# Split weights of a gated linear stage kept in DRAM and read back; the first block by plain products; no arithmetic on GpSimd

## The chip, the cores and the metric

The kernel runs on one core of one Trainium2 chip. The metric is device time in microseconds (us), the median of several executions; one more execution was taken by the hardware profiler. The engines are named as in the profile: PE (TensorE matmul), PEld (its weight load), DVE (VectorE), ACT (ScalarE), POOL (GpSimd) and SP (SyncE, which issues most DMAs here).

## What is computed

Linear attention with a per-head norm, then a mixture of eight experts of which each token takes one, then a gated linear unit. 4608 tokens of 512 features go through all of it, in float32.

```python
def _attn_ref(q, k, v, g_norm):
    kv = np.einsum('bhsd,bhse->bhde', k, v)
    out = np.einsum('bhsd,bhde->bhse', q, kv)
    rms = np.sqrt(np.mean(out * out, axis=-1, keepdims=True) + 1e-06)
    return (out / rms * g_norm).astype(np.float32)
...
def _moe_ref(x, modality_id, w_gate, modality_bias, w1, w2):
    logits = x @ w_gate + modality_bias[modality_id]
    e_idx = np.argmax(logits, axis=1)
    ...
        h = np.maximum(x[mask] @ w1[e], 0.0)
        out[mask] = gate_w[mask, None] * (h @ w2[e])
...
def _moe2_ref(x, w_gate, w_val, w_out):
    gate = 1.0 / (1.0 + np.exp(-(x @ w_gate)))
    val = x @ w_val
    return (gate * val @ w_out).astype(np.float32)
```

The last function is the stage that the change is about, the gate/value stage: w_gate and w_val are 512 x 1536, w_out is 1536 x 512.

## The kernel before

**Stages.** Attention comes first (to about 160 us). Then the expert stage, `run(0, NSURE)`: 22 items of one or two tiles of 128 tokens, four steps each, in which PE multiplies by pieces of w1 and w2 that ACT and DVE have split just before. Beside it, `Decode` turns the three float64 weights of the last stage into float32 and stores them in DRAM as `w_d`. Then the gate/value stage: 6 blocks (NB) of 768 tokens in two halves of 384 columns (HC), and in each block 12 units (NJ), one for each 128 of the 1536 inner features. Units are numbered 0 to 71. Unit 0 runs at the end of the expert stage (`gv_first`), before the branch at L954; the others run in the loop at L1151.

**Splits.** A float32 product is made as three float32r products. Each operand is split into hi (ACT copies it to float32r) and lo (a subtract of hi from the operand); then hi·hi, hi·lo and lo·hi are added in PSUM.

**A unit.** `glu_unit` (L627) makes gate and value of 128 inner features for 768 tokens by a scheme with seven products of half the depth in place of eight. That needs sums of the operands: of the weights (`sum_w`, four sums on POOL, L616) and of the tokens (`y_steps`, four sums on POOL, L578), and sums of the results, which DVE makes from PSUM (L638). A product is six matmuls of 384 columns (L634 to L636): 42 for a unit. Weights for unit s + 1 are split during unit s, in four groups (`split_wg`: ACT L624, DVE L625); the raw rows come from `w_d` by one read of 512 KB for each unit (L986). The split weights of a unit are used once and made again in each of the six blocks.

**Output steps.** `ready_o` (L1002) splits 128 rows of w_out, read from `w_d` (ACT L1010, POOL L1011), and the finished product gm (ACT L1015, DVE L1016, `gl`); `out_step` (L1020) then issues nine matmuls of 512 columns. In units 1 to 12 there is one for each unit, from unit 13 on two; the last 14 stand at the end, behind unit 71.

**Order.** The order is written out by hand. `glu_unit` calls `at(p)` after each of its products, and `prepare(s, p)` (L1095) holds what every engine does there for later units; each engine keeps to the order in which its instructions are issued. In units 10 and 11 of a block, the next block's y operands are made in seven steps (s1 to s7: ACT L573, DVE L574, POOL L578). In block 0 the last eight of the 36 decoding jobs run too (`Late`, units 2 to 9; their last add is on POOL, L1080). SP issues its DMAs in program order, and one that waits holds up all behind it.

**The way into the stage.** The last 16 steps of the expert stage (`later(q, ...)`, q = 0 to 15) also prepare unit 0 and block 0: rows of y are read, each row's gate is gathered by POOL (`number`), ACT multiplies by it (`weigh`, steps 5 to 7), PE transposes (`flip`, steps 6 to 11, ACT copies to `yraw`), POOL sums the weights (step 6), ACT and DVE split them (`group0`, steps 11 to 14), and `steps0` makes the seven y operands in steps 12 to 15: POOL copies hi (L571), DVE subtracts lo (L574), POOL sums (L578).

Of the kernel before, what the change touches and what calls it, by code (L numbers as in the profile page):

```python
# [73 lines left out]
def attention_moe_glu_kernel(  # L74
# [487 lines left out]


    y11, y12, y21, y22 = (yraw[:, 2 * k:2 * k + 2, h, :] for k in range(2) for h in range(2))
    free_y, Y = [], {}

    def split_y(b, n, src, first=False):

        hl = free_y.pop(0)
        if first:  # L570
            nc.gpsimd.tensor_copy(out=hl[0], in_=src)  # L571
        else:
            nc.scalar.activation(out=hl[0], in_=src, func=ACTF.Copy)  # L573
        nc.vector.tensor_tensor(out=hl[1], in0=src, in1=hl[0], op=ALU.subtract)  # L574
        Y[b, n] = hl

    def sum_y(out, in0, in1, op):
        nc.gpsimd.tensor_tensor(out=out, in0=in0, in1=in1, op=op)  # L578

    def y_steps(b, first=False):  # L580


        def s1():
            split_y(b, 3, y22, first)
            sum_y(y22, y22, y12, ALU.subtract)

        def s2():
            split_y(b, 1, y11, first)
            sum_y(y12, y12, y11, ALU.subtract)
            sum_y(y11, y22, y11, ALU.add)  # L590

        def s3():
            split_y(b, 6, y11, first)

        def s4():
            split_y(b, 7, y22, first)

        def s5():
            split_y(b, 2, y21, first)
            sum_y(y21, y21, y11, ALU.subtract)  # L600

        def s6():
            split_y(b, 4, y21, first)

        def s7():
            split_y(b, 5, y12, first)
# [583 lines left out]
```

## Time and profile before

| | us |
|---|---|
| median of 3 executions | 1651.11 (1649.55 to 1652.71) |
| the profiled execution | 1653.95 |
| its span, first to last instruction | 1652.2 |
| PE busy | 1484.2 |
| DVE busy | 1211.9 |
| ACT busy | 839.1 |
| POOL busy | 748.4 |
| mean granted clock of PE | 0.955 of full speed |

Times in the rows below are us from the span's start. Matmuls are pipelined: the duration of one is its latency, so the pace of PE is read from the distance between starts. "Busy" counts instructions that overlap once. Releasers of a wait are inferred from semaphores.

### The profile page before, as it was taken

How to read it: one execution, taken by the hardware profiler on the slowest of the kernel's cores; microseconds unless marked ns; L12 is line 12 of the kernel's file. 1: busy time of each engine (PE TensorE's matmuls, PEld its weight loads, DVE VectorE, ACT ScalarE, POOL GpSimd, SP SyncE). 2: the span in 40 equal slices, each digit the busy share in tenths (PEclk: the TensorE clock that was granted, in tenths of full speed). 3: DMA queues.
4: the chain of work that ended last, by engine and by line, in shares of the span. 5: the costliest groups of instructions: out<-in, count | busy, mean ns of one | idle time of the engine just before them, and what ended most of it. 6: DMA issues, size and time to landing. Idle time of an engine off the chain costs nothing.

```text
span 1652.2 us, 25283 instructions
## 1 busy us (share of the span) xinstructions
PE 1484.2 (90%) x9361; PEld 1350.6 (82%) x9361; DVE 1211.9 (73%) x1766; ACT 839.1 (51%) x1492; POOL 748.4 (45%) x777
## 2 busy tenths in 40 slices
PE   6993999999999987788789989997999799989996
PEld 6882899999999976677679888987998798879984
DVE  2658778888887877577677786778777877877764
ACT  3755555555555566244344454454455445544443
POOL 1121122222222234455466665666566667565545
PEclk9986999999999998799799999999999999999999
DMA  9957687758866773323223323332333233222312
GB/s 298 338 192 267 189 302 270 255 187 320 282 225 234 255 279 133 110 90 135 96 79 127 116 77 107 116 108 74 116 112 106 77 122 119 87 83 96 116 52 101
DMA packets 122816, 266.29 MB, mean 161 GB/s; under 512 B 17728, under 2 KB 38464, under 8 KB 121664
## 3 DMA queue, kind: packets, MB, share of 16 engines
q1 hardware_dynamic: 108480, 228.01, 41.3%
q0 software_dynamic: 11488, 36.27, 6.2%
q8 instruction: 75, 1.23, 0.3%
q10 hardware_dynamic: 2720, 0.35, 0.2%
q14 instruction: 53, 0.43, 0.1%
HBM read 245.24 MB, written 40.32 MB: 173 GB/s over the span
## 4 chain that ended last, share of the span: by engine, by line
PE 70%; DVE 8%; POOL 7%; issue 5%; ACT 4%; DMA 4%; SPq 0%; ACTq 0%; POOLq 0%; another core or an unknown queue 0%; DVEq 0%
PE gv L634 9%; PE gv L636 8%; PE gv L635 8%; PE ac L1031 4%; PE ac L1032 4%; PE ac L1030 4%; PE py L810 4%; PE py L809 4%; PE py L811 4%; PE ph L772 4%; PE ph L771 4%; PE ph L770 4%; DVE wt L625 2%; PE kv L248 2%; PE ops L285 2%
## 5 line engine op out<-in xcount | busy, mean ns | idle before, releaser
L625 DVE TENSOR_TENSOR wt<-rows,wt 128x512 fp32r<-128x512 f32 (+1 forms) x284 | 235.0, 832 | 109.7 <-ACT wt L624 108.1
L1011 POOL TENSOR_TENSOR wol<-wo,woh 128x512 fp32r<-128x512 f32 x144 | 193.1, 1343 | 262.7 <-ACT woh L1010 260.7
L616 POOL TENSOR_TENSOR rows<-rows 128x256 f32<-128x256 f32 x288 | 250.1, 889 | 37.0 <-DMA rows<-w_d 24.5
L634 PE MATMUL gv<-half,wt 128*128 128x384 f32 x590 | 204.8, 347 | 29.3 <-DVE u L638 10.7
L636 PE MATMUL gv<-half,wt 128*128 128x384 f32 x590 | 200.9, 340 | 0.3 <-DVE wt L625 0.3
L635 PE MATMUL gv<-half,wt 128*128 128x384 f32 x590 | 200.4, 340 | 0.0
L819 POOL DMA_INDIRECT y_d<-y,sidx x40 | 48.0, 1201 | 299.3 <-issue 130.8
L1031 PE MATMUL ac<-wol,gh 128*128 128x512 f32 x432 | 172.7, 400 | 10.3 <-POOL wol L1011 10.3
L1016 DVE TENSOR_TENSOR gl<-gm,gh 128x384 fp32r<-128x384 f32 x144 | 168.8, 1173 | 14.3 <-ACT gh L1015 14.3
L1032 PE MATMUL ac<-woh,gl 128*128 128x512 f32 x432 | 172.3, 399 | 0.0
L1030 PE MATMUL ac<-woh,gh 128*128 128x512 f32 x432 | 169.7, 393 | 0.1
L624 ACT ACTIVATE wt<-rows 128x512 fp32r<-128x512 f32 (+1 forms) x284 | 158.1, 570 | 18.2 <-POOL rows L616 12.7
L770 PE MATMUL ph<-xh,w1h 128*128 128x256 f32 x576 | 166.6, 289 | 0.8 <-ACT xh L753 0.8
L772 PE MATMUL ph<-xl,w1h 128*128 128x256 f32 x576 | 163.8, 284 | 0.0
L771 PE MATMUL ph<-xh,w1l 128*128 128x256 f32 x576 | 163.7, 284 | 0.0
L634 PEld LDWEIGHTS gv<-half,wt 128*128 128x128 f32 x590 | 112.9, 191 | 41.3 <-DVE gm L638 15.6
L666 ACT ACTIVATE s<-s 128x384 f32<-128x384 f32 x71 | 37.4, 526 | 194.5 <-DVE s L638 194.5
L810 PE MATMUL py<-w2l,hh 128*128 128x512 f32 x320 | 126.8, 396 | 0.8 <-DVE w2l L732 0.8
L809 PE MATMUL py<-w2h,hh 128*128 128x512 f32 x320 | 126.7, 396 | 0.1
L811 PE MATMUL py<-w2h,hl 128*128 128x512 f32 x320 | 125.4, 392 | 0.0
L635 PEld LDWEIGHTS gv<-half,wt 128*128 128x128 f32 x590 | 113.0, 192 | 2.2
L636 PEld LDWEIGHTS gv<-half,wt 128*128 128x128 f32 x590 | 112.7, 191 | 1.0 <-DVE wt L625 1.0
(258 smaller groups left out, 3790.6 us busy)
## 6 DMA issues: line engine op xcount, KB each, us to landing
half<-in_moe_w_dram SPq DMA_DIRECT2D x24, 2048.0 KB
rows<-w_d SPq DMA_DIRECT2D x72, 512.0 KB
wo<-w_d SPq DMA_DIRECT2D x144, 256.0 KB
w1r<-in_moe_w_dram SPq DMA_DIRECT2D x11, 2048.0 KB
w2r<-in_moe_w_dram SPq DMA_DIRECT2D x11, 2048.0 KB
kt<-in_k_dram SPq DMA_DIRECT2D x8, 1152.0 KB
vt<-in_v_dram SPq DMA_DIRECT2D x8, 1152.0 KB
x_d<-o SPq DMA_DIRECT2D x8, 1152.0 KB
```

The lines of the kernel that those rows point to most:

```text
L616: nc.gpsimd.tensor_tensor(out=r[:, o], in0=r[:, a], in1=r[:, c], op=op)
L625: nc.vector.tensor_tensor(out=t[:, 1, 0:z - a], in0=r[:, a:z], in1=t[:, 0, 0:z - a], op=ALU.subtract)
L634: nc.tensor.matmul(out=o, lhsT=wh, rhs=yh[:, c, :], start=first and c == 0, stop=False, skip_group_check=True)
L635: nc.tensor.matmul(out=o, lhsT=wh, rhs=yl[:, c, :], start=False, stop=False, skip_group_check=True)
L636: nc.tensor.matmul(out=o, lhsT=wl, rhs=yh[:, c, :], start=False, stop=last and c == 1, skip_group_check=True)
L770: nc.tensor.matmul(out=o, lhsT=bh[:, c, cs], rhs=hi[:, c, 0:n], start=(c == 0), stop=False)
L771: nc.tensor.matmul(out=o, lhsT=bl[:, c, cs], rhs=hi[:, c, 0:n], start=False, stop=False)
L772: nc.tensor.matmul(out=o, lhsT=bh[:, c, cs], rhs=lo[:, c, 0:n], start=False, stop=(c == KC - 1))
L1011: nc.gpsimd.tensor_tensor(out=lo, in0=src, in1=hi, op=ALU.subtract)
L1030: nc.tensor.matmul(out=o, lhsT=gh[:, cs], rhs=wh, start=(k == 0), stop=False)
L1031: nc.tensor.matmul(out=o, lhsT=gh[:, cs], rhs=wl, start=False, stop=False)
L1032: nc.tensor.matmul(out=o, lhsT=gl[:, cs], rhs=wh, start=False, stop=(k == NJ - 1))
```

## The change

- `w_d` holds a unit's rows in another order (`store`), so that the plain product and the sums find theirs.
- Two new sets of DRAM buffers: `wt_d`, one for each of the 12 weight pieces, with the seven split operands (hi and lo of each), and `wo_d`, with the split rows of w_out.
- Block 0 (units 0 to 11) runs through `glu_plain`: eight products, no sums, gate straight into the sigmoid. Its y operands are hi and lo of the transposed rows, made by `flip0` from PSUM (ACT and DVE). The four weight pieces of a unit are split (two groups), and the three that the later scheme uses as they are go to `wt_d` (`group`, s < NJ).
- Block 1 reads those three back (`load_wt`, n = 3), makes the four sums on DVE (`sum_w`), splits them (two groups) and stores them.
- Blocks 2 to 5 only read: 7 split operands for each unit, and for each output step split rows of w_out from `wo_d`. The rows of w_out are split and stored once, in units 1 to 12; the lo half is made by DVE.
- Sums of y, the last add of late decoding and the lo half of w_out move from POOL to DVE. POOL keeps the gathers, the scatters and the small copies of indices.
- In the last 16 steps of the expert stage `weigh` moves from steps 5 to 7 to steps 7 to 9, the flips from 6 to 11 to 12, 13 and 15, and the two weight groups stand in steps 10 and 14.

```diff
+    wt_d = [dram.tile([128, 7, 2, 256], F32, name=f"wt_d{j}") for j in range(F2 // 128)]
+    wo_d = [dram.tile([128, 2, DM], F32, name=f"wo_d{j}") for j in range(F2 // 128)]
...
-                lo = 512 * m + 128 * c
+                lo = (0, 128, 256, 384, 768, 896, 512, 640)[4 * m + c]
...
+    def flip0(i, src, ps):
+
+        turn(src, ps)
+        h, cs = i // HT, slice((i % HT) * 128, (i % HT) * 128 + 128)
+        hi, lo = (yA[0][:, 2 * h:2 * h + 2, z, :, cs] for z in range(2))
+        ps = ps.rearrange("p (k c) f -> p k c f", k=2)
+        nc.scalar.activation(out=hi, in_=ps, func=ACTF.Copy)
+        nc.vector.tensor_tensor(out=lo, in0=ps, in1=hi, op=ALU.subtract)
...
+    def split_w2(src, dst):
+
+        nc.scalar.activation(out=dst[:, :, 0, :], in_=src, func=ACTF.Copy)
+        nc.vector.tensor_tensor(out=dst[:, :, 1, :], in0=src, in1=dst[:, :, 0, :], op=ALU.subtract)
+
+    def glu_plain(w, y, bank, tmp, gm, at):
...
+        for h in range(2):
+            g = gm(h)
+            pg, sg = bank("ad"[h]), tmp("s1" if h == 0 else "s2")
+            product((0, 1), h, pg)
+            nc.scalar.activation(out=sg, in_=pg, func=ACTF.Sigmoid)
+            at((1, 2)[h])
+            if h:
+                at(4)
+                at(5)
+            pv = bank("bc"[h])
+            product((3, 2), h, pv)
+            nc.vector.tensor_tensor(out=g, in0=sg, in1=pv, op=ALU.mult)
+            if h == 0:
+                at(6)
+                at(7)
+        at(3)
...
-            later(5 + i // 2, lambda i=i: weigh(0, i, y0(i)))
-            later(6 + i, lambda i=i: flip(i, y0(i), ptx.tile([128, KC, 128], F32, tag="xt", name="xtp")))
-        later(2, lambda: nc.sync.dma_start(out=rows0[:, 0:4], in_=w_rows(0)))
-        later(6, lambda: sum_w(rows0))
...
+            later(7 + i // 2, lambda i=i: weigh(0, i, y0(i)))
+            later(12 + i // 2 + (i > 3), lambda i=i: flip0(i, y0(i), ptx.tile([128, KC, 128], F32, tag="xt", name="xtp")))
+        later(2, lambda: nc.sync.dma_start(out=rows0, in_=w_rows(0)))
+        for g in range(2):
+            later(10 + 4 * g, lambda g=g: split0(g))
...
+        def sum_y(out, in0, in1, op):
+            nc.vector.tensor_tensor(out=out, in0=in0, in1=in1, op=op)
...
+        def load_wt(s):
+            if NJ <= s < NU:
+                n = 3 if s < 2 * NJ else 7
+                nc.sync.dma_start(out=wts[s % 2][:, 0:n].bitcast(F32), in_=wt_d[s % NJ][:, 0:n])
...
+            if NJ <= s < 2 * NJ:
+                r = rows[s % 2]
+                t = wsum[s] = ws.tile([128, 4, 256], F32, tag="wsum", name="wsum", bufs=1)
+                add = lambda o, a, c, op: nc.vector.tensor_tensor(out=o, in0=a, in1=c, op=op)
...
         def group(s, g):
-            if s < NU:
-                split_wg(rows[s % 2], g, wts[s % 2][g])
+            if s < NJ:
+                split_w2(rows[s % 2][:, 2 * g:2 * g + 2], wts[s % 2][:, 2 * g:2 * g + 2])
+                if g:
+                    nc.sync.dma_start(out=wt_d[s][:, 0:3], in_=wts[s % 2][:, 0:3].bitcast(F32))
+            elif s < 2 * NJ:
+                a = 3 + 2 * g
+                split_w2(wsum[s][:, 2 * g:2 * g + 2], wts[s % 2][:, a:a + 2])
+                if g:
+                    nc.sync.dma_start(out=wt_d[s % NJ][:, 3:7], in_=wts[s % 2][:, 3:7].bitcast(F32))
...
+            if (b, h) == (0, 0):
+                raw_o[s, z] = ws.tile([128, DM], F32, tag="wo", name="wo", bufs=2)
+                nc.sync.dma_start(out=raw_o[s, z], in_=w_d[k // 4][:, k % 4, 1024:1536])
+            else:
+                split_o[s, z] = ws.tile([128, 2, DM], F32R, tag="wos", name="wos", bufs=4)
+                nc.sync.dma_start(out=split_o[s, z].bitcast(F32), in_=wo_d[k][:, :, :])
...
+                nc.scalar.activation(out=t[:, 0], in_=src, func=ACTF.Copy)
+                nc.vector.tensor_tensor(out=t[:, 1], in0=src, in1=t[:, 0], op=ALU.subtract)
+                nc.sync.dma_start(out=wo_d[k][:, :, :], in_=t.bitcast(F32))
...
-                nc.gpsimd.tensor_tensor(out=self.f, in0=self.z, in1=self.p, op=ALU.add)
+                nc.vector.tensor_tensor(out=self.f, in0=self.z, in1=self.p, op=ALU.add)
...
             if spot == 0:
+                load_wt(s + 1)
                 load_rows(s + 2)
                 decode_late(s)
+                sum_w(s + 1)
```

How the order of instructions moves is shown at three places. The first is DVE in the last steps of the expert stage, from the flips of step 12 (in the changed kernel) to those of step 15; w1l, w2l and hl are the expert weights' and activations' subtracts, L574 and L571 the y operands of block 0, L625 and L579 the weights of unit 0. Before:

```order
L625 TENSOR_TENSOR d_raw<-rows_2027,d_raw 128x512
L574 TENSOR_TENSOR half_7572<-yraw,half_7572 128x768
L732 TENSOR_TENSOR w1l<-w1r_2034,w1h 128x1024
L732 TENSOR_TENSOR w2l<-w2r_2035,w2h 128x1024
L797 TENSOR_TENSOR hl<-htp,hh 128x2x128
L625 TENSOR_TENSOR d_raw<-rows_2027,d_raw 128x512
L574 TENSOR_TENSOR half_7572<-yraw,half_7572 128x768 x2
L732 TENSOR_TENSOR w1l<-w1r_2034,w1h 128x1024
```

and in the changed kernel:

```order
L571 TENSOR_TENSOR half_7553<-xtp,half_7553 128x2x2x128 x2
L719 TENSOR_TENSOR w1l<-w1r_2057,w1h 128x1024
L719 TENSOR_TENSOR w2l<-w2r_2058,w2h 128x1024
L784 TENSOR_TENSOR hl<-htp,hh 128x2x128
L571 TENSOR_TENSOR half_7553<-xtp,half_7553 128x2x2x128 x2
L719 TENSOR_TENSOR w1l<-w1r_2057,w1h 128x1024
L719 TENSOR_TENSOR w2l<-w2r_2058,w2h 128x1024
L784 TENSOR_TENSOR hl<-htp,hh 128x2x128
L579 TENSOR_TENSOR d_raw<-rows_2051,d_raw 128x2x256
```

The subtracts that waited for POOL's copies and sums (L574) are gone, and the subtracts from PSUM (`xtp`) stand in their place. The second place is DVE in unit 29, in the middle of block 2. Before:

```order
L625 TENSOR_TENSOR wt_8559<-rows_2027,wt_8559 128x512
L638 TENSOR_TENSOR u_11804<-u_11804,gv 128x384
L1016 TENSOR_TENSOR gl<-gm_8567,gh 128x384
L638 TENSOR_TENSOR u_11805<-u_11804,gv 128x384
L625 TENSOR_TENSOR wt_8560<-rows_2027,wt_8560 128x512
L625 TENSOR_TENSOR wt_8561<-rows_2027,wt_8561 128x512
L638 TENSOR_TENSOR gm_8570<-u_11804,gv 128x384
L625 TENSOR_TENSOR wt_8562<-rows_2027,wt_8562 128x256
L638 TENSOR_TENSOR gm_8567<-u_11805,gv 128x384
L1016 TENSOR_TENSOR gl<-gm_8573,gh 128x384
L638 TENSOR_TENSOR s_11807<-u_11804,gv 128x384
L667 TENSOR_TENSOR gm_8570<-s_11806,gm_8570 128x384
```

and in the changed kernel:

```order
L625 TENSOR_TENSOR u_11480<-u_11480,gv 128x384
L1077 TENSOR_TENSOR gl<-gm_8562,gh 128x384
L625 TENSOR_TENSOR u_11481<-u_11480,gv 128x384
L625 TENSOR_TENSOR gm_8565<-u_11480,gv 128x384
L625 TENSOR_TENSOR gm_8562<-u_11481,gv 128x384
L1077 TENSOR_TENSOR gl<-gm_8568,gh 128x384
L625 TENSOR_TENSOR s_11483<-u_11480,gv 128x384
L654 TENSOR_TENSOR gm_8565<-s_11482,gm_8565 128x384
```

The four weight subtracts are gone from between the sums. The third place is SP's queue for two units in the blocks from 2 on. Before:

```order
L986 DMA rows_2027<-w_d_73 128x1024
L1050 DMA yr<-y_d 128x528
L1000 DMA wo<-w_d_73 128x512 x2
L986 DMA rows_8554<-w_d_73 128x1024
L1050 DMA yr<-y_d 128x528
```

and in the changed kernel:

```order
L1024 DMA wt_8556<-wt_d_78 128x3584
L1112 DMA yr<-y_d 128x528
L1060 DMA wos<-wo_d_91 128x1024
L1060 DMA wos<-wo_d_92 128x1024
L1024 DMA wt_8555<-wt_d_79 128x3584
```

The read of a unit's rows becomes a read of its split weights, three and a half times as long, one unit ahead instead of two; each read of w_out's rows is twice as long.

## Rows read from the trace of the kernel before

**Rows 1.** The page, busy time, share of the span and instructions of each engine.
```profile
PE 1484.2 (90%) x9361; PEld 1350.6 (82%) x9361; DVE 1211.9 (73%) x1766; ACT 839.1 (51%) x1492; POOL 748.4 (45%) x777
```

**Rows 2.** Stretches: length, busy PE, PEld, DVE, ACT, POOL, PEclk, DMA share, GB/s.
```profile
757.00:771.00 14.00, 11.35 (x56) 10.58 (x55) 9.63 (x16) 5.80 (x13) 6.96 (x8) 0.88 0.39 133
...
1501.56:1513.20 11.64, 11.64 (x62) 10.63 (x61) 8.83 (x14) 5.17 (x12) 5.82 (x7) 1.00 0.29 92
...
1122.70:1136.62 13.92, 12.15 (x64) 11.02 (x63) 13.86 (x16) 6.61 (x14) 9.15 (x6) 1.00 0.18 58
1136.62:1157.12 20.50, 13.19 (x60) 11.73 (x59) 16.00 (x20) 9.01 (x18) 13.50 (x12) 0.92 0.20 64
```

**Rows 3.** Timeline of PE, block 5 (start, duration); last, a block-0 transpose in the chain.
```profile
1594.07 0.33 PE L634 MATMUL gv<-w1r,wt 128*128 128x384 f32 x1
...
1596.67 0.39 PE L1030 MATMUL ac<-woh,gh 128*128 128x512 f32 x1
...
1598.76 0.33 PE L634 MATMUL gv<-half,wt 128*128 128x384 f32 x1
...
738.64 0.44 PE tr L555 x4
```

**Rows 4.** Waits in 1122.7 to 1157.12 us: total, times, longest.
```profile
PE gv L634 <- DVE gm L638: 6.2, 2, 4.4
```

**Rows 5.** Waits in 595 to 665 us.
```profile
PE ph L765 <- DVE w1l L732: 9.8, 3, 7.7
...
PE htp L794 <- ACT hs L779: 6.1, 2, 5.6
...
ACT d_raw L550 <- DMA gate_t<-gate_d,oid: 5.0, 2, 3.4
```

**Rows 6.** Line L634 (times of first and last start), and timeline of ACT, step 12.
```profile
L634 PE MATMUL gv<-half,wt x590: 331/334/689, 683.9 to 1604.5; 128*128 128x384 f32 x197
...
L634 PE MATMUL ph<-half,d_raw x6: 335/335/425, 665.6 to 669.4; 128*128 128x384 f32 x6
...
640.36 1.05 ACT L731 ACTIVATE w1h<-w1r 128x1024 fp32r<-128x1024 f32 x1
```

**Rows 7.** Timeline of ACT: a unit's first read of PSUM, units 12, 24 and 60.
```profile
848.73 0.49 ACT L642 ACTIVATE u<-gv 128x384 f32<-128x384 f32 x1
...
1002.50 0.49 ACT L642 ACTIVATE u<-gv 128x384 f32<-128x384 f32 x1 [0.81 <-PE gv L636]
...
1465.57 0.49 ACT L642 ACTIVATE u<-gv 128x384 f32<-128x384 f32 x1 [0.80 <-PE gv L636]
```

**Rows 8.** Lines on DVE and POOL: ns shortest/median/longest, first and last start.
```profile
L1016 DVE TENSOR_TENSOR gl<-gm,gh x144: 544/1206/3465, 693.2 to 1639.3; 128x384 fp32r<-128x384 f32 x144
...
L625 DVE TENSOR_TENSOR wt<-rows,wt x284: 410/692/3192, 683.9 to 1590.5; 128x512 fp32r<-128x512 f32 x142
...
L638 DVE TENSOR_TENSOR u<-u,gv x142: 539/542/556, 692.7 to 1597.5; 128x384 f32<-128x384 f32 x142
...
L578 POOL TENSOR_TENSOR yraw<-yraw x24: 1800/2000/2734, 646.8 to 1454.0; 128x768 f32<-128x768 f32 x24
...
L574 DVE TENSOR_TENSOR half<-yraw,half x25: 943/959/2570, 645.8 to 1458.8; 128x768 fp32r<-128x768 f32 x25
...
L754 DVE SCALAR_TENSOR_TENSOR xl<-xtp,gcol,xh x40: 739/750/752, 163.5 to 631.6; 128x512 fp32r<-128x512 f32 x40
...
L732 DVE TENSOR_TENSOR w1l<-w1r,w1h x44: 1216/1218/1836, 187.4 to 658.7; 128x1024 fp32r<-128x1024 f32 x44
```

**Rows 9.** Stretches (columns as in rows 2), expert stage, large loads alone.
```profile
395.00:401.00 6.00, 6.00 (x42) 5.51 (x41) 5.48 (x8) 4.42 (x6) 1.15 (x2) 1.00 1.01 406
```

**Rows 10.** The chain that ended last, in the tail: start, duration.
```profile
1630.43 2.80 DMA wo<-w_d
...
1640.30 0.49 PE ac L1031
```

More of the change, by code (lines that the diff above doesn't have):

```diff
@@ L561, in y_rows @@
         return y_d[r:r + 128, :]
[L564 to L606, printed above, removed]
-        return s1, s2, s3, s4, s5, s6, s7
+    yA = []
@@ new lines, in glu_plain, with product @@
+    def glu_plain(w, y, bank, tmp, gm, at):
+        def product(ga, h, o):
+            for k in range(2):
+                wh, wl = (w(ga[k])[:, z, :] for z in range(2))
+                yh, yl = y(h, k)
+                for c in range(2):
+                    cs = slice(c * 128, c * 128 + 128)
+                    nc.tensor.matmul(out=o, lhsT=wh[:, cs], rhs=yh[:, c, :], start=k == 0 and c == 0, stop=False)
+                    nc.tensor.matmul(out=o, lhsT=wh[:, cs], rhs=yl[:, c, :], start=False, stop=False)
+                    nc.tensor.matmul(out=o, lhsT=wl[:, cs], rhs=yh[:, c, :], start=False, stop=k == 1 and c == 1)
+        for h in range(2):
[14 more added lines that the diff above has]
+        at(3)
@@ L860, in y0, with split0 @@
             return early_y[i // 2][:, i % 2]
[L862 to L863 removed]
         wt0 = []
[L867 removed]
+        def split0(g):
             wt0.append(dec.tile([128, 2, 2, 256], F32R, tag="d_raw", name="d_raw", bufs=4))
[L869 to L871 removed]
+            split_w2(rows0[:, 2 * g:2 * g + 2], wt0[g])
+            if g == 0:
+                nc.sync.dma_start(out=wt_d[0][:, 0:2], in_=wt0[0].bitcast(F32))
+            else:
+                nc.sync.dma_start(out=wt_d[0][:, 2:3], in_=wt0[1][:, 0:1].bitcast(F32))
+        later(12, lambda: yA.append(mw[0].tile([128, 5, 2, 2, HC], F32R, tag="half0", name="half0")))
         for i in range(2 * HT):
@@ L982, in attention_moe_glu_kernel, with hold_y @@
         raw_o, split_o, split_g, acc = {}, {}, {}, {}
-        def load_rows(s):
-            if s < NU:
-                nc.sync.dma_start(out=rows[s % 2][:, 0:4], in_=w_rows(s % NJ))
-        def sums(s):
-            if s < NU:
-                sum_w(rows[s % 2])
-        def group(s, g):
-            if s < NU:
-                split_wg(rows[s % 2], g, wts[s % 2][g])
+        y11, y12, y21, y22 = (yraw[:, 2 * k:2 * k + 2, h, :] for k in range(2) for h in range(2))
+        free_y = []
+        def hold_y(t, lo=0):
+            free_y.extend((t[:, k, 0], t[:, k, 1]) for k in range(lo, t.shape[1]))
@@ new lines, in split_y, with y_steps, s1, s2 @@
+        def split_y(b, n, src):
+            hl = free_y.pop(0)
+            nc.scalar.activation(out=hl[0], in_=src, func=ACTF.Copy)
+            nc.vector.tensor_tensor(out=hl[1], in0=src, in1=hl[0], op=ALU.subtract)
+            Y[b, n] = hl
+        def sum_y(out, in0, in1, op):
+            nc.vector.tensor_tensor(out=out, in0=in0, in1=in1, op=op)
+        def y_steps(b):
+            def s1():
+                split_y(b, 3, y22)
+                sum_y(y22, y22, y12, ALU.subtract)
+            def s2():
+                split_y(b, 1, y11)
+                sum_y(y12, y12, y11, ALU.subtract)
+                sum_y(y11, y22, y11, ALU.add)
+            def s3():
+                split_y(b, 6, y11)
+            def s4():
+                split_y(b, 7, y22)
+            def s5():
+                split_y(b, 2, y21)
+                sum_y(y21, y21, y11, ALU.subtract)
+            def s6():
+                split_y(b, 4, y21)
+            def s7():
+                split_y(b, 5, y12)
+            return [s1, s2, s3, s4, s5, s6, s7]
```

106 lines of the change are left out of this document (49 added, 57 removed).

## The prediction

> **What bounds the kernel now.** I read the page's busy shares first, then the execution by stretches, then who waits for whom in the bad stretches. On the whole PE is busy 90% of the span and DVE 73% [rows 1], but the stages differ. In the middle of the last block a unit takes 11.64 us, PE is busy all of it at the full granted clock, and DVE only 8.83 [rows 2]: there PE is the bound. The spacing of its matmuls says the same: from 1594.07 to 1596.67 us stand 15 of 384 columns, 0.173 us each, and from there to 1598.76 nine of 512 columns, 0.232 each [rows 3]. A unit has 42 of the first and 18 of the second: 42 × 0.173 + 18 × 0.232 = 11.45. Nothing that relieves another engine makes such a unit shorter.
>
> Three stretches are not like that. In block 0 a unit takes some 14 us, with PE busy four fifths of it at a granted clock of 0.88, so part of the time at the lower of its two levels [rows 2]. At the end of each block but the last, while the next block's y operands are made, the last two units take 13.9 and 20.5 us, DVE is busy all of the first, and PE waits 6.2 us in one group alone for a DVE sum that frees a bank [rows 2, 4]. Between the expert stage and the gate/value stage (605 to 665 us) PE waits 9.8 us for w1l and 6.1 for an ACT relu, and ACT 5.0 for gathered gates [rows 5]. From the first matmul of unit 1 (683.9 [rows 6]) block 0 lasts to 847.7, six matmuls before the first ACT read of unit 12 at 848.73; block 1 takes 153.8, blocks 2 to 4 463.1 together, and block 5 runs from 1465.57 on [rows 7].
>
> **Why DVE is slow there.** The same subtract gl takes 544 ns at best, 1206 in the median and 3465 at worst; the weight subtract 692 in the median and 3192 at worst; but the add that reads one operand from PSUM takes 539 to 556 always [rows 8]. What stretches are DVE instructions with two SBUF inputs, and in these stretches POOL adds and subtracts (its y sums take 2.0 us each [rows 8]). With POOL's arithmetic gone I take what they need undisturbed: 0.55 for 384 columns, 0.69 for 512, 0.41 for 256, 0.945 for 768 [rows 8]. Were POOL not the cause, gl would stay at its median of 1.21 and a y subtract would now and then take 2.57; that is part of the first rival. The Trainium skill (SBUF — State Buffer, "SBUF: two separate sides") says that a DVE instruction with two SBUF inputs and a GpSimd instruction that reads SBUF take one port pair in turn, each for its whole length. The rows agree with it: by that rule the sum is the one below, and without it the time is the first rival's.
>
> **The change, part by part.**
>
> *The way into the stage.* Weighing moves two steps later, so most of ACT's 5.0 us for gates goes: −4. In steps 12 to 15 the seven POOL casts, the POOL sums and seven DVE subtracts go; two flips come into each of steps 12, 13 and 15, with a DVE subtract from PSUM of 512 columns, 0.75 each [rows 8]. DVE's work for these steps is then seven weight subtracts of 1.22 [rows 8], four small ones at under 0.75, six at 0.75 and one of 0.69: 16.7 at most. Before, the four steps took from 640.4, the ACT split of w1 that opens step 12, to unit 0's first product at 665.6 [rows 6], 25 us. I take −9. Unit 0 has 48 matmuls, 8.3 us, but none of the waits between its sums, which made it 10 us: −2. Together −15; the bounds are −5 (a new wait takes half) and −20.
>
> *Block 0, units 1 to 11.* The cost of plain products: eight instead of seven, 6 × 0.173 = 1.04 us per unit, 12.5 over the block, all on PE. A unit is then 48 × 0.173 + 9 × 0.232 = 10.4, and 0.44 more in six units with transposes [rows 3]: 117 for eleven. DVE falls below that: two products at 0.55, two weight subtracts and the wo subtract (moved from POOL) at 0.69, gl 0.55, and late decoding with its last add now on DVE, at most five of 0.69: 7.2 of 10.4. The product needs no chain of sums u, u3, s before its sigmoids. I add 7: 3 in unit 1, because the store of its split weights stands on SP ahead of the loads of rows(2) and wo and waits for DVE; 2 at the block's end; 2 for small slips. 124 against 163.8: −40. Bounds: −47 (nothing but PE) and −20 (units of 12.7).
>
> *Block 1.* On DVE four POOL sums of 256 columns (0.41 each) replace two of the four weight subtracts; the wo subtract is gone except in its first unit. Leaving the y work aside, DVE has five adds of 0.54, two products, two subtracts of 0.69, two gl and 1.6 of sums: 7.9 of 11.64. At PE's pace the block is 12 × 11.64 and six times 0.3 for transposes, 141.5; I add 2.5 for the block's end: 144, −10.
>
> *Blocks 2 to 5.* Weight and wo splitting go from DVE, ACT and POOL; DVE has about 5 us of a unit. The ending units carry seven y subtracts and four y sums (from POOL to DVE, no row on DVE; the subtract of the same shape, 0.945, is the near bound, POOL's 2.0 the far one; I take 0.945): 10.4 us in two units of 23.3 in all, on top of about 10. So the stall nearly goes: 1.5 a block. Blocks 2 to 4: 3 × 143 = 429, −34 (bounds −20 and −39). Block 5 prepares no y and stands at PE's pace already: 0.
>
> *The reads that pay for it.* A unit of blocks 2 to 5 reads 1.84 MB of split weights and 1.05 of wo, with y and output 3.15 MB, 271 GB/s; block 1 moves 3.7 MB with its stores, 314. In the expert stage large loads ran at 406 GB/s with every DMA engine busy [rows 9]. The weights' read is issued when PE leaves the unit before, since it overwrites those weights, and has one unit: 1.84 MB at 406 is 4.5 us, and a read of 256 KB alone landed in 2.80 [rows 10], so some 7 of 11.64 us. Hidden, cost 0. SP's queue waits there for PE, with y and wo reads behind it; these are due a unit later.
>
> *The tail.* From the last gate/value matmuls (1604.5 [rows 6], and two more) to 1641.2, one matmul after the last of [rows 10], PE does 14 output steps, of 9 × 0.232 = 2.09 us: 29.2. Now each pair waits for a 2.80 us read, ACT, and POOL [rows 10]; four buffers and no split let it run at PE's pace: −7 (bounds −2 and −8).
>
> **Sum.** −15 − 40 − 10 − 34 − 7 = −106 from the profiled execution's 1653.95: 1548. That execution lies 2.84 above the median, so 1545.
>
> **Rivals.**
> 1. *The y preparation stalls as before*: the longer DVE times stay, or DVE's queue, which now holds the sums too, is late. Against it: a unit of blocks 2 to 5 goes from 8.83 us of DVE work to about 5, which leaves room for it. 5 us a block more over four blocks, +20: 1565.
> 2. *Block 0 is bound by hand-overs*, not by PE: ACT and DVE must split wo within the one product before its output step needs it, behind late decoding on DVE. For it: such a queue rules block 0 now. +20: 1565; with rival 1, 1585.
> 3. *Read-back starves PE; slower than before.* Place: the weights' read, which can't start before the unit before has ended. Units 1 to 71 move some 228 MB; before they took 921 us, and way in and tail save 22, so the point of decision is 228 MB in 943 us, 242 GB/s. At 225 GB/s units last 1015: 1653.95 − 22 + 94 − 3 = 1723. For it: the second half moves 92 GB/s now with DMA at 0.29 of its time [rows 2], which at full time would be 317, and nothing there shows more; against it, the 406.
> 4. *The POOL chain was not what held PE*, so way in and block ends keep half of their waits: inside the forecast's own range.
>
> **How the numbers follow.** Forecast 0.60 (1530 to 1562), rivals 1 and 2 0.14 each, both 0.04, rival 3 0.04, better than 1530 0.04. The range 1530 to 1585 takes in all but the last two. A change under 0.2% can't be told from none; faster than that 0.95, the same 0.01, slower 0.04.
>
> **What would show it.** Right: units of blocks 1 to 5 at 11.6 to 12 us up to the blocks' ends, gl near 0.55 throughout, block 0 near 10.5 to 11 a unit, no PE wait for a DMA on wt, DMA near 0.7 of its time, first unit of block 0 some 15 us earlier. Wrong: PE waiting for wt at the start of a unit (rival 3), for gl, wos or a DVE add inside block 0 (rival 2), units 10 and 11 of a block still above 14 us (rival 1).

## The result and the profile after

The changed kernel takes **1541.13 us** (median of 4 executions, 1536.33 to 1547.54) against 1651.91 of the kernel before in the same comparison: a ratio of **0.933, 95% interval 0.929 to 0.937**. 1545 was predicted, 1530 to 1585 the range. The profiled execution is the longest of the four: 1547.54, span 1545.7.

The page's busy line, against [rows 1]:

```profile
PE 1456.7 (94%) x9433; PEld 1340.9 (87%) x9433; DVE 920.3 (60%) x1553; ACT 656.7 (42%) x1108; POOL 227.6 (15%) x306
```

DVE lost 292 us and POOL 521, PE only 28. Four stretches of the changed kernel, columns as in [rows 2]: a unit of block 0, one in the middle of block 5, units 34 and 35 (a block's end).

```profile
745.11:755.96 10.85, 10.85 (x63) 10.40 (x62) 6.41 (x12) 4.83 (x9) 1.38 (x2) 1.00 0.97 342
1485.23:1496.72 11.49, 11.49 (x62) 10.70 (x61) 4.68 (x9) 2.26 (x6) 0.00 (x0) 1.00 0.81 311
1060.46:1072.94 12.48, 11.77 (x62) 10.63 (x61) 9.08 (x14) 3.73 (x9) 0.00 (x0) 1.00 0.64 238
1072.94:1085.40 12.46, 11.75 (x62) 10.61 (x61) 9.85 (x15) 6.05 (x12) 0.00 (x0) 1.00 0.59 228
```

In the first two PE is busy throughout, at the full granted clock. The block's end still holds 0.7 us of idle PE a unit, against 1.8 and 7.3 in [rows 2]. Two lines of DVE (ns shortest/median/longest) answer to [rows 8]; a y sum now stands on DVE:

```profile
L1077 DVE TENSOR_TENSOR gl<-gm,gh x144: 549/552/625, 685.0 to 1532.5; 128x384 fp32r<-128x384 f32 x144
...
L979 DVE TENSOR_TENSOR yraw<-yraw x20: 951/957/959, 782.3 to 1363.2; 128x768 f32<-128x768 f32 x20
```

The spread of gl is gone: longest 0.625 us, where it was 3.465. From unit 12's first read to the end PE's list of waits has DVE adds alone, and no DMA (total, times, longest):

```profile
PE gv L621 <- DVE gm L625: 5.7, 8, 0.7
PE gv L621 <- DVE u L625: 3.0, 2, 2.0
```

Three first reads on ACT answer to [rows 7] (units 12, 24 and 60):

```profile
797.50 0.49 ACT L629 ACTIVATE u<-gv 128x384 f32<-128x384 f32 x1 [0.77 <-PE gv L623]
...
942.96 0.49 ACT L629 ACTIVATE u<-gv 128x384 f32<-128x384 f32 x1
...
1370.30 0.49 ACT L629 ACTIVATE u<-gv 128x384 f32<-128x384 f32 x1
```

The start of unit 1, SP and then PE (start, duration, in brackets the idle time before and what ended it):

```profile
670.84 0.33 SPq L1019 DMA_DIRECT2D rows<-w_d  x1
...
675.61 0.69 PE L590 MATMUL gv<-half,wt 128*128 128x384 f32 x1 [5.95 <-ACT wt L578]
676.09 0.52 PE L591 MATMUL gv<-half,wt 128*128 128x384 f32 x1
676.41 0.61 PE L592 MATMUL gv<-half,wt 128*128 128x384 f32 x1
```

Unit 1's rows are asked for only when the expert stage is over; PE stands still 5.95 us and then runs at 0.32 us a matmul, not 0.173: the lower clock level.

Cut at the same marks, five profiles compare as follows (us). The first mark is ACT's copy of y for the sixth-last item of the expert stage, ahead of the last 16 steps, which the change edits. move_alone, as_block1 and late_ystep are runs explained below.

| stretch | before | move_alone | as_block1 | changed | late_ystep |
|---|---|---|---|---|---|
| to the mark | 568.8 | 565.5 | 563.5 | 573.6 | 564.5 |
| mark to unit 0's first matmul | 96.8 | 92.3 | 87.1 | 86.0 | 85.5 |
| to unit 1's first matmul | 18.3 | 19.1 | 16.1 | 16.0 | 15.8 |
| units 1 to 11, to unit 12's first read | 164.8 | 165.6 | 121.9 | 121.9 | 122.2 |
| block 1 | 153.8 | 146.4 | 145.5 | 145.5 | 144.0 |
| blocks 2 to 4 | 463.1 | 440.2 | 436.0 | 427.3 | 423.2 |
| block 5, to unit 71's first read | 129.2 | 126.4 | 126.4 | 126.4 | 126.4 |
| rest | 57.4 | 51.6 | 49.2 | 49.0 | 49.3 |
| span | 1652.2 | 1607.1 | 1545.7 | 1545.7 | 1531.0 |

Up to the mark these kernels do the same work in the same order, yet that stretch varied from 562.5 to 573.6 us over the profiles of this study. So stages are compared below, not spans, where a few us matter.

### The profile page after: what moved, and what is told of

Same layout as the page of the kernel before. It is cut to its first block, busy times and chain, and to the rows that moved or that the text cites. A ratio compares the mean times of both kernels' runs of the same rounds, so it can differ in the third digit from the quotient of the medians.

```text
span 1545.7 us, 24066 instructions
## 1 busy us (share of the span) xinstructions
PE 1456.7 (94%) x9433; PEld 1340.9 (87%) x9433; DVE 920.3 (60%) x1553; ACT 656.7 (42%) x1108; POOL 227.6 (15%) x306
## 4 chain that ended last, share of the span: by engine, by line
PE 50%; DVE 4%; ACT 1%; DMA 1%; issue 1%; POOL 0%; POOLq 0%; SPq 0%; ACTq 0%; DVEq 0%
PE gv L621 9%; PE gv L623 9%; PE gv L622 9%; PE ac L1093 6%; PE ac L1094 6%; PE ac L1092 6%; PE gv L590 2%; PE gv L591 2%; PE gv L592 2%; DVE yraw L979 1%; PE tr L556 1%; DVE half L975 1%; DMA rows<-w_d 1%; DVE gm L625 1%; DVE w1r L975 1%
## 5 line engine op out<-in xcount | busy, mean ns | idle before, releaser
L625 DVE TENSOR_TENSOR gm<-u,gv 128x384 f32<-128x384 f32 x120 | 65.6, 553 | 180.9 <-PE gv L623 180.9
L1094 PE MATMUL ac<-wos,gl 128*128 128x512 f32 x432 | 171.2, 396 | 0.0
L1093 PE MATMUL ac<-wos,gh 128*128 128x512 f32 x432 | 170.9, 396 | 0.2 <-DVE wos L1072 0.2
L1092 PE MATMUL ac<-wos,gh 128*128 128x512 f32 x432 | 168.5, 390 | 0.1
L621 PE MATMUL gv<-half,wt 128*128 128x384 f32 x408 | 140.1, 343 | 8.7 <-DVE gm L625 5.7
L623 PE MATMUL gv<-half,wt 128*128 128x384 f32 x408 | 137.2, 336 | 0.0
L622 PE MATMUL gv<-half,wt 128*128 128x384 f32 x408 | 137.0, 336 | 0.0
L757 PEld LDWEIGHTS ph<-xh,w1h 128*128 128x128 f32 x576 | 110.9, 193 | 2.5 <-ACT xh L740 1.2
L758 PEld LDWEIGHTS ph<-xh,w1l 128*128 128x128 f32 x576 | 111.0, 193 | 1.4
L759 PEld LDWEIGHTS ph<-xl,w1h 128*128 128x128 f32 x576 | 110.9, 192 | 0.3 <-DVE xl L741 0.3
L1103 POOL DMA_INDIRECT out_dram<-ot,to x36 | 36.2, 1006 | 487.0 <-DVE ot L1098 295.4
L625 DVE TENSOR_TENSOR s<-u,gv 128x384 f32<-128x384 f32 x60 | 33.3, 554 | 117.2 <-PE gv L623 114.7
L1094 PEld LDWEIGHTS ac<-wos,gl 128*128 128x128 f32 x432 | 81.3, 188 | 18.1 <-DVE gl L1077 0.8
L1093 PEld LDWEIGHTS ac<-wos,gh 128*128 128x128 f32 x432 | 81.3, 188 | 14.5 <-DVE wos L1072 0.6
```

Of the source, the lines that this page charges most:

```text
L621: nc.tensor.matmul(out=o, lhsT=wh, rhs=yh[:, c, :], start=first and c == 0, stop=False, skip_group_check=True)
L622: nc.tensor.matmul(out=o, lhsT=wh, rhs=yl[:, c, :], start=False, stop=False, skip_group_check=True)
L623: nc.tensor.matmul(out=o, lhsT=wl, rhs=yh[:, c, :], start=False, stop=last and c == 1, skip_group_check=True)
L757: nc.tensor.matmul(out=o, lhsT=bh[:, c, cs], rhs=hi[:, c, 0:n], start=(c == 0), stop=False)
L758: nc.tensor.matmul(out=o, lhsT=bl[:, c, cs], rhs=hi[:, c, 0:n], start=False, stop=False)
L759: nc.tensor.matmul(out=o, lhsT=bh[:, c, cs], rhs=lo[:, c, 0:n], start=False, stop=(c == KC - 1))
```

## Experiments

Theory 1, the prediction's: GpSimd's arithmetic stretched DVE, and DVE made PE wait. Theory 2: the change helps because DVE and ACT have less to do.

### GpSimd's work moved to DVE, nothing else (move_alone)

```diff
-        nc.gpsimd.tensor_tensor(out=out, in0=in0, in1=in1, op=op)
+        nc.vector.tensor_tensor(out=out, in0=in0, in1=in1, op=op)
```

The same in `sum_w`, in `ready_o`, in the late decoding's last add and in the first block's copies of y, on the kernel before.

> The kernel before with one part of the change alone: every sum, difference and copy that GpSimd made for the stage (weight sums, y sums, the lo part of wo, the end of the late decoding) is made by VectorE; block 0 stays with the seven products, nothing is kept in DRAM. Theory 1 (VectorE was late because GpSimd's arithmetic stretched its two-input instructions): gl falls from a mean of 1.17 us to about 0.55, and although VectorE gets 4 x 0.42 + 2 x 0.68 = 3.0 us more work a unit (about 11.0 of a unit's 11.5 us) the time falls: blocks 2 to 4 about 145 to 150 us each instead of 154, block 0 about 140 to 155 instead of 164.8, in all 1580 to 1610 us. Theory 2 (VectorE was simply given too much work, and the change helps because it no longer splits the weights anew): moving work onto VectorE makes it later, and the time is no better than before, 1650 us or more.

Measured: 1610.04 us, ratio 0.976 (0.972 to 0.979). Units 1 to 11, a block's last two units (10 and 11 of block 2), and the wait that stands first in units 1 to 11:

```profile
676.88:842.49 165.61, 131.57 (x593) 122.09 (x594) 128.30 (x248) 64.46 (x130) 7.39 (x13) 0.83 0.33 107
1105.40:1119.95 14.55, 13.04 (x67) 11.58 (x66) 13.85 (x24) 6.61 (x14) 0.00 (x0) 1.00 0.26 74
1119.95:1135.47 15.52, 12.03 (x61) 10.57 (x61) 14.64 (x26) 8.80 (x18) 0.00 (x0) 1.00 0.23 68
```

```profile
PE gv L634 <- DVE u L638: 33.0, 10, 6.6
```

From block 1 on theory 1 holds: DVE has more instructions, gl is at 0.55, and a block takes 146.4 to 147.1 us in place of 154. In block 0 it fails: 165.6, no gain, where 140 to 155 was expected. PE waits there 33.0 us for a DVE sum (29.7 in the kernel before) while DVE is busy 77% of the time, so DVE has time enough in all; that speaks for the order of its queue rather than its load. Unit 6 of move_alone shows such a wait, DVE first and then PE:

```profile
748.29 0.43 DVE L1074 TENSOR_SCALAR w2r<-w2r 128x512 int32<-128x512 int32 x1
...
750.67 0.69 DVE L1080 TENSOR_TENSOR w2r<-w2r 128x512 f32<-128x512 f32 x1
...
753.41 0.54 DVE L638 TENSOR_TENSOR u<-u,gv 128x384 f32<-128x384 f32 x1
```

```profile
754.01 0.69 PE L634 MATMUL gv<-w1r,wt 128*128 128x384 f32 x1 [3.30 <-DVE u L638]
```

Late decoding (five instructions, 3.0 us), two splits, gl and another add stand without a gap ahead of the add that PE waits for. No run changes that order by itself.

### Blocks 2 to 5 prepared as block 1 is (as_block1)

```diff
-            if NJ <= s < 2 * NJ:
+            if NJ <= s < NU:
                 r = rows[s % 2]
```

`load_rows` and `group` go on to NU too, `load_wt` reads three operands for all units. The sums are made and split anew in each unit, not read back.

> The changed kernel with blocks 2 to 5 prepared as block 1 is: 3 of 7 weights are read back as they stand, the four sums are made by VectorE and split anew in each unit. The DRAM copy of the sums is not read. Theory 1 (the gain came from GpSimd's arithmetic being gone, and block 1 at 145.5 us shows it): blocks 2 to 4 take about 145.5 us in place of 142.4, block 5 one or two us more, the time is 1541 + 11 = about 1552 us. Theory 2 (the gain came from not splitting anew): blocks 2 to 4 go back to about 154 us each, the time is 1575 us or more.

Measured: 1546.85 us (1545.03 to 1548.81). By stages blocks 2 to 4 cost 8.6 us more than in the changed kernel (436.0 against 427.3), all of it in the last two units of each block (13.7 and 14.1 in place of 12.5); blocks 1 and 5 and the rest are the same. So reading back the sums is worth some 9 us of the 111.

### GpSimd arithmetic that nothing waits for (idle_gpsimd, idle_block0)

```diff
+            for i in range(4):
+                nc.gpsimd.tensor_tensor(out=junk[:, 1, 0:256], in0=junk[:, 0, 0:256], in1=junk[:, 0, 256:512], op=ALU.add)
+            for i in range(2):
+                nc.gpsimd.tensor_tensor(out=junk[:, 1], in0=junk[:, 0], in1=junk[:, 0], op=ALU.subtract)
```

About as many as the kernel before made there, issued at the start of each unit: from unit 12 on (idle_gpsimd) or in units 1 to 11 alone (idle_block0).

> The changed kernel, with arithmetic on GpSimd that nothing waits for: from block 1 on, in every unit, 4 sums of 128x256 and 2 differences of 128x512 on a tile of their own, as many and as large as the kernel before made there. Theory 1 (GpSimd's arithmetic stretches VectorE's instructions with two SBUF inputs): gl rises from 0.55 us to 0.8 to 1.2 us on the mean with single ones over 2 us, VectorE's adds with one PSUM input stay at 0.55, and the block ends lengthen again; as VectorE has room now (67 of 142 us busy in a block), the time rises only by 5 to 30 us, to 1546 to 1571. Theory 2 (only the work taken away counts): gl stays at 0.55, the time within 0.2% of the changed kernel's 1541 us.

> The changed kernel with GpSimd arithmetic that nothing waits for in the units of block 0 alone (4 sums of 128x256 and 2 differences of 128x512 in each of 11 units). It tells whether block 0's 43 us came from the stopped arithmetic or from the plain products. Theory A (block 0 gained because the plain products leave VectorE and the hand-overs little to do): units 1 to 11 stay within 122 to 135 us, the time is 1541 to 1555 us. Theory B (it gained because GpSimd is silent): units 1 to 11 go back towards 164 us, the time to 1570 us or more.

Measured: 1554.12 us (1552.81 to 1556.01) and 1555.79 (1552.66 to 1563.46). DVE lines of idle_gpsimd, then its block 1 and block 2:

```profile
L1077 DVE TENSOR_TENSOR gl<-gm,gh x144: 548/554/1354, 675.9 to 1537.8; 128x384 fp32r<-128x384 f32 x144
...
L625 DVE TENSOR_TENSOR u<-u,gv x120: 539/547/555, 792.2 to 1504.4; 128x384 f32<-128x384 f32 x120
...
L655 DVE TENSOR_TENSOR gm<-s,gm x60: 545/892/1393, 801.1 to 1513.9; 128x384 f32<-128x384 f32 x60
```

```profile
789.23:946.57 157.34, 144.09 (x737) 131.53 (x736) 115.24 (x189) 55.03 (x107) 83.83 (x96) 0.98 0.77 282
946.57:1089.55 142.98, 141.27 (x746) 130.55 (x745) 75.21 (x121) 41.97 (x84) 82.93 (x96) 1.00 0.71 265
```

The stretch is shown by itself: with nothing waiting for GpSimd, DVE instructions with two SBUF inputs grow (gm, median 0.892; in the changed kernel 0.559) and those with one operand in PSUM do not (u, 0.555 at most). Its price went with DVE's load: 11.9 us in block 1, where DVE is busy 66% of the changed kernel's time, and under 1 us a block in blocks 2 to 4, where it is 47%; block 1 also differs in what DVE does, so two stages do not show that the load alone sets it. gl's mean was 0.684, less than the 0.8 to 1.2 expected.

Block 0 with silent GpSimd takes 121.9 us, with the idle arithmetic 136.1, just over the bound of theory A:

```profile
666.44:802.55 136.11, 127.64 (x659) 118.42 (x660) 91.15 (x122) 50.39 (x94) 75.21 (x80) 0.95 0.72 243
```

So of block 0's 43 us, 29 come with the plain products, and the fewer splits that belong to them, even when GpSimd works beside them, and 14 only when it is silent. Moving its arithmetic to DVE gave nothing there by itself (move_alone).

### The sums alone on GpSimd (wsums_gpsimd, ysums_gpsimd)

wsums_gpsimd is as_block1 with the weight sums made there, issued one unit earlier, behind product 5, into two buffers; ysums_gpsimd is the changed kernel with the y sums made there.

```diff
-                add = lambda o, a, c, op: nc.vector.tensor_tensor(out=o, in0=a, in1=c, op=op)
+                add = lambda o, a, c, op: nc.gpsimd.tensor_tensor(out=o, in0=a, in1=c, op=op)
...
-            nc.vector.tensor_tensor(out=out, in0=in0, in1=in1, op=op)
+            nc.gpsimd.tensor_tensor(out=out, in0=in0, in1=in1, op=op)
```

> The kernel as_block1 with one thing moved: the four weight sums of each unit of blocks 1 to 5 are made by GpSimd instead of VectorE, one unit earlier (as the kernel before had them). Same work in all; VectorE has 1.7 us less of it a unit. Theory 1 (GpSimd's arithmetic stretches VectorE's two-input instructions): in spite of the smaller load the block ends get no shorter, gl's mean is 0.62 to 0.7 us, and the time is that of as_block1 or up to 1% more, 1546 to 1562 us. Theory 2 (VectorE's own work sets the block ends): the blocks shrink from 145.5 to 143 to 144 us, the time falls to 1535 to 1542 us.

> The changed kernel with the four y sums (128x768) of each block's end put back on GpSimd, nothing else. Theory 1: each of them takes 1.8 us or more on GpSimd in place of 0.96 on VectorE, stands in the chain of the y preparation and stretches VectorE's splits beside it; the two last units of a block go from 12.5 us each to 14 to 17, so five blocks cost 15 to 45 us: 1556 to 1586 us. Theory 2 (VectorE only gets 4 us less to do at each block's end): the two units fall to 12 us, 1536 to 1541 us.

Measured: 1575.43 us (1571.47 to 1575.69) and 1543.43 (1540.55 to 1545.67). Both are off theory 1's numbers. The first costs 28.6 us against as_block1, more than either theory gave (the profiles differ by 23.9 in blocks 1 to 5 and by 4.4 ahead of the mark), and GpSimd's timeline in unit 25 says where:

```profile
951.68 0.99 POOL L1103 DMA_INDIRECT out_dram<-ot,to  x1 [0.28 <-POOL to L1102]
952.68 0.29 POOL L1102 COPY to<-oid 128x1 int32<-128x1 int32 x1
953.24 0.98 POOL L1103 DMA_INDIRECT out_dram<-ot,to  x1 [0.28 <-POOL to L1102]
954.25 0.75 POOL L1034 TENSOR_TENSOR wsum<-rows 128x256 f32<-128x256 f32 x1
```

```profile
ACT wt L578 <- POOL wsum L1034: 3.1, 1, 3.1
```

The sums stand behind the scatters of finished output rows, ACT waits 3.1 us for them (waits of 950 to 970 us), and the unit takes 15.2 us:

```profile
952.26:967.45 15.19, 13.33 (x62) 12.21 (x61) 6.57 (x12) 3.41 (x9) 8.48 (x11) 0.89 0.67 230
```

PE is idle for 1.86 us of it, and its matmuls, 11.49 us in the same unit of as_block1, take 13.33 at a granted clock of 0.89: the lost clock costs as much as the wait. Two units in each block, each after the scatters of a half, are longer (by 1.6 to 3.7 us) and make up the difference in the blocks: it is GpSimd's queue more than the stretch.

In the second run a y sum takes 1.85 us in place of 0.96, yet the last two units of a block of 2 to 4 take 24.94 us together, as in the changed kernel. That is one gain and one loss of 1.0 us, not an absence of effect. Units 34 and 35 of ysums_gpsimd:

```profile
1053.35:1064.84 11.49, 11.49 (x62) 10.71 (x61) 7.76 (x11) 3.73 (x8) 5.53 (x3) 1.00 0.65 248
1064.84:1078.29 13.45, 11.75 (x62) 10.62 (x61) 8.90 (x14) 6.05 (x12) 1.97 (x2) 1.00 0.55 217
```

In unit 34 the two sums no longer stand on DVE ahead of the add that PE needs, and the stall is gone; in unit 35 ACT and then DVE wait for the longer sum, and PE 1.7 us behind them. From block 0's first matmul in the loop to unit 12's first read this run takes 124.2 us (121.9 in the changed kernel) and in block 1 147.5 (145.5).

### One split moved behind an add (late_ystep)

```diff
-                    for p, n in ((1, 1), (6, 1), (7, 1), (2, 1), (4, 1)):
+                    for p, n in ((1, 1), (6, 1), (7, 1), (2, 1), (5, 1)):
```

In unit 10 of a block likewise, spot 5 in place of 4.

> The changed kernel with one y step in each of a block's two last units moved from behind product 4 to behind the output step after product 5. In the changed kernel VectorE's split of that step (0.95 us) stands ahead of the add that reads product 5, and TensorE's product 3, which adds to the same bank, waits 0.7 us for it in each of these units. If that order is what lengthens the block ends: the two units fall from 12.48 us each to 11.5 to 11.8, five blocks give 6 to 10 us, 1531 to 1535. If the y chain itself is what ends last there (as the run ysums_gpsimd suggests, where the sum of the two units stayed at 24.94 us): no change, 1541.

Measured: **1532.75 us** (1530.22 to 1533.54), ratio 0.927 (0.925 to 0.929): faster than both kernels. The two units take 12.0 and 11.6 us. In the changed kernel, units 34 and 35, the first line; in late_ystep, 1045 to 1075 us, the second:

```profile
PE gv L621 <- DVE gm L625: 1.4, 2, 0.7
```

```profile
PE gv L621 <- DVE gm L625: 0.2, 1, 0.2
```

So what ended last at the block's end was one add in each of the two units, held up by the y step issued ahead of it. In unit 35 that is a 0.95 us split; in unit 34 it is a split and two sums, 2.9 us (DVE, changed kernel):

```profile
1067.20 0.95 DVE L975 TENSOR_TENSOR half<-yraw,half 128x768 fp32r<-128x768 f32 x1
1068.06 1.95 DVE L979 TENSOR_TENSOR yraw<-yraw 128x768 f32<-128x768 f32 x2
1069.93 0.55 DVE L625 TENSOR_TENSOR gm<-u,gv 128x384 f32<-128x384 f32 x1
```

By stages blocks 1 to 4 gain 5.5 us. The two profiles differ by another 9.6 us ahead of unit 0, where profiles vary anyway, so how much of the 8.4 us between the medians is the edit's is known only by stages.

### More reads beside the read-back (more_dma1, more_dma3)

```diff
+        def load_more(s):
+            if s >= 2 * NJ:
+                for t in more[:3]:
+                    nc.sync.dma_start(out=t, in_=w_rows(s % NJ))
...
+                load_more(s)
```

Three loads of 512 KB at the start of each unit from block 2 on, into tiles that nothing uses (more_dma3), or one (more_dma1, `more[:1]`).

> As more_dma3 with one extra load of 512 KB a unit in place of three: about 266 + 46 = 311 GB/s in blocks 2 to 5. In more_dma3 the stages stretched by 16 us at 386 GB/s, with a DMA share of 0.99. If there is a limit near 386 and nothing below it: units of 11.49 us, blocks 2 to 4 at 427.3 us as in the changed kernel. If transfers delay each other already below it: 430 us or more.

> The changed kernel with three more loads of 512 KB in each unit of blocks 2 to 5, from DRAM into tiles that nothing uses; about 137 GB/s beside the 266 that these units move, 403 in all, which is what the window at 395 us of the kernel before showed at its highest (406). Theory 1 (read-back is hidden while the engines' rows show room: DMA share 0.71): the units keep 11.49 us up to that rate, and the time rises by 0 to 15 us. Rival (the read-back already runs near what the queue can sustain, some 300 GB/s): a unit takes 4.6 MB / 300 = 15.4 us, 48 units add about 185 us, 1725 us. In between, at 360 GB/s a unit takes 12.9 us and the time is about 1608.

Measured: 1539.91 us (one execution) and 1557.39 (1551.47 to 1561.33). Blocks 2 to 4 of either:

```profile
935.72:1363.01 427.29, 423.01 (x2234) 391.76 (x2233) 201.43 (x363) 125.89 (x251) 43.80 (x72) 1.00 0.82 310
```

```profile
940.48:1379.07 438.59, 425.45 (x2234) 391.28 (x2233) 201.52 (x363) 125.92 (x251) 44.56 (x72) 1.00 0.99 388
```

In more_dma3 PE's longest wait in that stretch is a new one:

```profile
PE ac L1099 <- DMA wos<-wo_d: 8.8, 9, 1.5
```

At 310 GB/s the three blocks take 427.3 us, as in the changed kernel at 266. At 388, with the DMA engines busy 0.99 of the time, they take 11.3 us more, and block 5 another 5.1. The read-back is hidden, with room for another 44 GB/s at least.

### Unit 1 prepared earlier (early_unit1, early_and_late, early_wo)

```diff
+        later(8, lambda: nc.sync.dma_start(out=rows1, in_=w_rows(1)))
+        later(9, lambda: nc.sync.dma_start(out=wo0, in_=w_d[0][:, 0, 1024:1536]))
+        later(15, lambda: nc.sync.dma_start(out=rows0, in_=w_rows(2)))
```

early_unit1 has the first line, and splits these rows beside unit 0's products; early_and_late adds the third and late_ystep's edit; early_wo has all.

> The changed kernel with unit 1's weights prepared earlier: their rows are loaded in the expert stage into a tile of their own (step 8 of the way in) and split while unit 0's products run, in the room that the change left free; before, that load was issued only after the expert stage had ended and TensorE stood still for 5.95 us. If the gap is that load: unit 1's first matmul comes 1 to 3 us after unit 0's stage ends (669.7 in the changed kernel's profile) in place of 5.95, TensorE's clock does not fall to 1.2 GHz for the 8 us behind it (matmuls 0.17 apart, not 0.32), and the time falls by 5 to 11 us to about 1533 (1530 to 1536). If the gap is the conditional block's own: no change, 1541.

> late_ystep and early_unit1 together, with the rows of unit 2 loaded early as well: in early_unit1 the gap of 5.95 us ahead of unit 1 went, and a wait of 3.8 us came in unit 1, where ScalarE's split of unit 2's rows (landed at 673.0) stands ahead of the copy that unit 1's output step needs. If that load was the next to come last: unit 0's first matmul to unit 12's first read takes 131 to 133 us in place of 137.9 (changed kernel) and 135.9 (early_unit1), and with the block ends 1525 to 1531 us in all. If some other wait takes its place, within 3 us of late_ystep alone.

> early_and_late with wo's first piece loaded in the expert stage too. In early_and_late the wait ahead of unit 1 had gone twice and come back once more: ScalarE's split of that piece waited 6.3 us for a load issued at 667.5, after the conditional block, and TensorE 4.3 us behind it, from where its clock fell again. If that is the last such load: unit 0's first matmul to unit 12's first read takes 131 to 133 us in place of 137.8, and the time is 1532 - 5 = 1527 us (1524 to 1529). If the transition is bound by the conditional block itself or by a further load: 136 us or more, 1531 to 1533.

Measured: 1539.47 us (1535.56 to 1542.54), 1532.2 (1531.28 to 1536.29) and 1533.04 (1530.06 to 1534.9): none measurably faster than what it started from. PE's waits from 655 to 790 us in early_unit1:

```profile
PE ac L1098 <- ACT gh L1082: 3.8, 1, 3.8
PE gv L592 <- ACTq L941: 1.3, 1, 1.3
```

The 5.95 us went, and a wait of 3.8 us came inside unit 1: ACT stands at a split of unit 2's rows, ahead of the copy that the output step needs. With these rows loaded early, ACT stood at wo's split and PE waited 4.3. With wo early as well that wait is 2.0; from unit 0's first matmul to unit 12's first read it is 134.5 us against 137.9 in the changed kernel. But in that profile the way from the mark to unit 0 took 89.3 us, where the nine kernels with the changed kernel's loads took 85.5 to 87.6, and the time did not fall. Whether its extra loads cause that is open.

## Why the prediction was right, and where it was off

| term | predicted | in the profile |
|---|---|---|
| way in, with unit 0 | −15 | −10.8 − 2.3 = −13.1 |
| block 0 | −40 | −42.9 |
| block 1 | −10 | −8.3 |
| blocks 2 to 4 | −34 | −35.7 |
| block 5 | 0 | −2.8 |
| tail | −7 | −8.4 |
| sum | −106 | −111.2 |
| ahead of the mark | | +4.8 |

1548 us was reckoned for the profiled execution, and it took 1547.54. So close a hit is luck: the stages gained 5.2 us more than the sum, and the part ahead of the mark, which the change leaves alone, took 4.8 more.

**The way in.** Right in size. Unit 0's first matmul is only 6.0 us earlier on the clock (659.64 against 665.6 [rows 6]), because this execution came 4.8 us later to the mark. Of the waits named, those for w1l and for the relu nearly went (595 to 665 us, changed kernel; 9.8 and 6.1 before [rows 5]), and ACT's for gates is no longer in the list:

```profile
PE ph L752 <- DVE w1l L719: 1.2, 3, 0.4
...
PE htp L781 <- ACT hs L766: 0.4, 1, 0.4
```

4.5 of the 10.8 us come in move_alone too, which leaves the steps where they were; how −4 and −9 share the rest no run shows.

**Block 0.** Right in size: a unit takes 10.85 us in the row above, 10.84 with transposes was reckoned. Units 1 to 11, before and changed:

```profile
683.90:848.73 164.83, 129.32 (x593) 118.94 (x594) 113.23 (x174) 64.67 (x130) 88.86 (x87) 0.85 0.32 108
675.60:797.50 121.90, 121.70 (x659) 116.17 (x660) 72.77 (x122) 50.46 (x94) 8.43 (x13) 0.98 0.79 271
```

PE's idle time falls by 35.3 us, to 0.2, and its busy time by 7.6, although the plain products add 11.4 (11 × 1.04) to it: its matmuls ran faster, at a granted clock of 0.98 in place of 0.85. The lower clock went with the waits. The reason given, that DVE's work falls below PE's, is part of it; the runs add that ending the stretch while DVE takes over GpSimd's work leaves block 0 where it was (move_alone), and that the plain products take away the sums for which PE waited. Of the 7 us added 4.9 were needed (121.9 − 117), some 3.4 of them in unit 1 (13.8 us to unit 2's first matmul, 10.4 in units 2 and 3). That the 3 put there came is luck: the reason given was a store ahead of loads, but PE is busy all through unit 1 and runs at the lower clock level behind the 5.95 us of standing still.

**Blocks 1 to 4.** Right. Of the 11.9 us that a block of 2 to 4 gained, about 7.6 come from GpSimd's arithmetic (move_alone), 2.9 from reading the sums back (as_block1 to the changed kernel), and 1.4, between those two, from reading back wo's split rows and three operands and what else differs there. These shares hold for this order of the steps; 7.6 is what is left after DVE has taken over GpSimd's work.

**Why DVE was slow.** Shown by idle_gpsimd: the stretch falls on DVE instructions with two SBUF inputs and spares those that read one operand from PSUM, as in [rows 8]. The Trainium skill (SBUF — State Buffer, "SBUF: two separate sides") lists a DVE instruction with two SBUF inputs as one that must share a port pair with GpSimd's reads, one of them blocked while the other runs. The trace agrees in kind: gm goes from 0.559 to 0.892 us in the median, u stays at 0.555 or less.

**The blocks' ends.** The stall was put at 1.5 us a block; it is 2.0 (24.94 − 2 × 11.49). The reason given, DVE's load, holds for the way there: the pair of units takes 34.4 us before, 30.1 in move_alone, 27.8 in as_block1 and 24.9 in the changed kernel, as DVE's instructions get shorter and then fewer. Of the 2.0 that stay, 1.4 are the order of a y step and an add (late_ystep); the prediction has a late DVE queue only in its rival 1.

**Block 5.** The step that failed is "Nothing that relieves another engine makes such a unit shorter". A middle unit fell from 11.64 to 11.49, also in move_alone: GpSimd's arithmetic cost some 0.15 us a unit there, and 11.45 had been worked out as PE's own pace. Another 1.1 of the 2.8 us came in the block's first unit (12.60 to 11.49).

**The rivals.** 1 did not come (ends at 12.5, gl at 0.55), 2 did not (block 0 at 10.85 a unit), 3 did not (more_dma1, more_dma3). For 3 the limit was taken as 406 GB/s; these transfers reach 388 over blocks 2 to 4. Rival 4 did not come: the stall at a block's end fell from 11.4 us (34.4 − 2 × 11.49) to 2.0. But it points the right way: with GpSimd's work moved and nothing else, 7.1 of the 11.4 stay, and block 0 keeps its waits.

## What to carry to other kernels

An engine's idle helper is not free: arithmetic on GpSimd made VectorE's instructions with two SBUF inputs longer, and cost most where VectorE had most to do. But moving that work to VectorE can also gain nothing, as in block 0, where the order of a queue seems to hold TensorE more than the length of its instructions. Before a gap is closed by more relief, look at what stands ahead of the releasing instruction in its queue: one step moved gave 5.5 us by stages here, and three loads moved forward gave none in the whole. A wait can cost twice, once as idle time and once as a lower clock behind it. Reading back results that were computed once is cheap as long as the DMA engines' share shows room: 0.71 of their time cost nothing, 0.99 did.
